# A fused RWKV recurrence and gated MLP on one core: the products of turned k with v cut from 64 to 48 weight columns, the order planned anew, PE gaps filled with longer products of a nearly empty tile, three constants moved to ScalarE

## The chip, the cores and the metric

The kernel runs on one core of a Trainium2 chip. The metric is device time in microseconds, from runs of the whole program. The work is spread over TensorE (PE; its weight loads are listed apart as PEld), VectorE (DVE), ScalarE (ACT), GpSimd (POOL) and the DMA queue of SyncE (SP).

## The reference

```python
def _attn_ref(r, k, v, w, u):
    B, H, S, D = r.shape                      # 4, 8, 768, 48
    state = zeros((B, H, D, D))
    for t in range(S):
        cur = einsum('bhd,bhe->bhde', u[None] * kt, vt)
        y[:, :, t] = einsum('bhd,bhde->bhe', rt, state + cur)
        state = wt[:, :, :, None] * state + einsum('bhd,bhe->bhde', kt, vt)

def _moe_ref(x, w_in, g_ln, w_sg, b_sg, w_out):   # x: (4, 768, 384), the 8 heads side by side
    h = gelu_tanh(x @ w_in)                       # w_in: (384, 1024)
    u, v = h[..., :512], h[..., 512:]
    v_n = (v - mean(v)) / sqrt(var(v) + 1e-6) * g_ln
    v_s = einsum('ts,bsd->btd', w_sg, v_n) + b_sg[None, :, None]   # w_sg: (768, 768)
    return x + (u * v_s) @ w_out                  # w_out: (512, 384)
```

`w_in` and `w_out` come as 64-bit floats and are split on the chip into two 32-bit parts.

## The kernel before

The recurrence is cut into 24 chunks of 128 time steps (4 batches of 6). In a chunk two heads share a tile: a head has 48 channels and takes 64 partitions, so that 16 of each 64 are empty. For each chunk `decays` makes running products of the decays with two scans on DVE (lines 456 and 461), `decays` and `decayed_k` multiply r and k by them (463 and 485, on DVE or POOL), and `turned_k` transposes k on PE (536) and copies it out of PSUM (311, tile `kt`). `own_weights` makes a step's own term (495 and 499 for the first six chunks, 510 to 515 after that) and spreads it over a diagonal into the tile `a` (522 on ACT, 524 on DVE or POOL). `products` makes two things in the PSUM tile `a_ps`: scores of k with r (550) and the turned k with v (553), which is what the chunk adds to the state. `masked` copies the scores into `a` (571, DVE), `state` and `decayed` carry the state on (586, 594, 605), and `outputs` multiplies `a` with v and the state with r (633 and 659), in the PSUM tile `y_ps`. A chunk's products and outputs are 64 by 64 tiles of PE, four side by side; from chunk 6 on the products of the next chunk stand between the two parts of a chunk's outputs.

The MLP follows on each half batch: `v_piece`, `u_piece`, `gate_piece`, `out_piece`, each a run of three products per pair of operands (725, 726, 727), with 128 weight columns and 384 or 512 moving columns.

All instructions are given out by a planner (`Plan`). Each piece of work is a generator that yields `Op`s with a cost per engine and what they wait for. `Plan.run` takes, for each engine, the ops that could start first and among those the one with the lowest rank; ranks are the tables `STEP`, `V`, `U`, `GATE`, `OUT` and `WEIGHT`, and `BIAS` is added to an engine's end when an op may go to several. So the tables fix the order on every engine, and the engine of many element-wise ops. On the chip each engine runs its instructions in this order and waits on semaphores.

Where the planner finds PE idle before 36 us, `keep_warm` puts products there that nobody reads: `ident` by `ident`, 128 columns each, in a PSUM tile that is free (976). At the start POOL makes the constants: `mask`, `diag` (390), `minus` (393) and `same` (394).

Of the kernel before, what the change touches and what calls it, by code (L numbers as in the profile page):

```python
# [38 lines left out]
    -49.59, -15.18, -14.63, -13.68, -11.2, -11.02, 0.94, 1.57, 6.83, 7.5, 7.96, 9.52, 17.35, 17.52, 18.44,  # L39
    20.96, 27.09, 21.08, 30.76, 30.42, 31.57, 41.12, 50.44, 52.07)  # L40
V = (
    -1.34, -0.42, -1.4, -16.57, -17.54, -16.72, -30.2, -1.18, 9.65, 3.42, -39.6, -58.94, -8.2, 47.77, -22.36,
    48.57, 27.83, 112.03, 39.65, 25.41, 38.54, -75.72, 34.43, 84.5)
U = (-10.14, -62.7, 73.58, 25.05, 43.25, -41.51, 3.24, -2.61)
GATE = (-5.38, 7.81, 4.64, 27.34, 89.18, 34.59, 11.76, 26.33)
OUT = (16.92, 42.66, 101.93, 26.86, 133.47, 116.26, 123.25, 158.13)
WEIGHT = {"v": -15.75, "u": -68.31, "sg0": -0.57, "sg1": -9.36, "out": -43.34, "g": 63.42}

HINTED = (mybir.EngineType.PE, mybir.EngineType.DVE, mybir.EngineType.SP)
BIAS = {"DVE": 0.32, "ACT": -0.03, "POOL": 0.34}  # L50
# [4 lines left out]
    (0, 'load_w'): -41.97, (0, 'load_kr'): -41.3, (1, 'load_w'): -38.98, (1, 'load_kr'): -16.05,  # L55
    (0, 'load_v'): -19.51}
# [91 lines left out]
class Plan:  # L148
# [62 lines left out]
    def run(self):  # L211
        while True:
# [13 lines left out]
            for e, c in best.items():  # L226
# [77 lines left out]
def rwkv_gmlp(ctx: ExitStack, tc: tile.TileContext, wpad, kr, vtok, ktok, vt, u, ucol, w_in, g_ln, w_sgT, b_sg, w_out, out):  # L304
# [47 lines left out]
    s_kt = slots("kt", 1, [NP, 128])  # L352
# [25 lines left out]
    nc.vector.memset(D2, 0.0)  # L378
    nc.gpsimd.memset(c.mhalf, -0.5)
# [147 lines left out]
    def turned_k(n):  # L527
# [9 lines left out]
        op = yield Op({"ACT": 0.48, "DVE": 0.58}, take=[s_kt], free=[m_], done=x.e_kt)  # L537
        x.kt, = op.got
        copy(op.e, x.kt.tile[0:m], kt_ps[0:m])

    def products(n, op):
# [9 lines left out]
        for p, c_, j in [(p, c_, j) for p in range(NP) for c_ in range(1 if last else 2) for j in range(2)]:  # L551
            h = 2 * p + j
            nc.tensor.matmul(ps[64 * j:64 * j + 64, c_, NP * T + p * T:NP * T + p * T + D],  # L553
                             kt[64 * c_:64 * c_ + 64, p, 64 * j:64 * j + 64],
# [6 lines left out]
    time = lambda n: {"PE": 0.78 if steps[n][1] == NC - 1 else 1.02}  # L561
# [59 lines left out]
    def outputs(n):  # L621
# [25 lines left out]
        plan.add(rank(n) - 50.0, look(y, e_look, op.seen))  # L647
        if n == N - 1:
# [518 lines left out]
```

## Time and profile before

| | |
|---|---|
| Time, median of 3 runs | 361.45 us (359.83 to 362.5) |
| Profiled execution, its own time | 360.21 us |
| Its span, first to last instruction | 358.5 us |
| PE busy | 346.5 us (97%), 4708 products |
| DVE busy | 274.8 us (77%) |
| ACT busy | 208.6 us (58%) |
| POOL busy | 80.3 us (22%) |
| DMA | 49.81 MB, mean 139 GB/s |

Busy times are those of the profiler; the ends of products are modelled, so the gap from one product's start to the next one's says more than a product's own length. A product of 32-bit floats shows as two records. An engine's idle time is shown with what ended it; "issue" means that the profile shows nothing that the engine waited for.

### The profile page before, as it was taken

The numbers are of one execution on the slowest core, as the hardware profiler recorded it, in microseconds if no ns is written. First come the engines' busy times: TensorE is split into PE (matmuls) and PEld (weight loads), VectorE is DVE, ScalarE is ACT, GpSimd is POOL, SyncE is SP. The second block draws the span as 40 slices with busy tenths as digits, with TensorE's granted clock in tenths as the row PEclk, the third lists the DMA queues.
The fourth block names the chain that finished last, engine by engine and source line by source line (L and its number), as shares of the span: only waits on it lengthen the run. The fifth ranks groups of instructions, "written<-read, shape, count | busy, mean of one in ns | idle before, by whom it ended". The sixth has DMA issues, their size and how long they took to land.

```text
span 358.5 us, 11334 instructions
## 1 busy us (share of the span) xinstructions
PE 346.5 (97%) x4708; PEld 317.4 (89%) x4708; DVE 274.8 (77%) x546; ACT 208.6 (58%) x545; POOL 80.3 (22%) x98
## 2 busy tenths in 40 slices
PE   5899999999999999999999999999999999999995
PEld 5778678898998888989999899998999989999994
DVE  6979998789999999989999877767642527345352
ACT  2868978884456677675644364667562588721010
POOL 7413320123454241443214020105000002000000
PEclk9989999999999999999999999999999999999998
DMA  7867777522466545633563614513224440010101
GB/s 249 307 192 228 233 239 247 163 100 76 115 192 215 186 146 190 205 116 126 157 205 123 199 52 140 160 69 117 102 66 153 133 145 3 0 44 24 44 24 71
DMA packets 23960, 49.81 MB, mean 139 GB/s; under 512 B 3808, under 2 KB 12768, under 8 KB 23904
## 3 DMA queue, kind: packets, MB, share of 16 engines
q1 hardware_dynamic: 23904, 49.04, 42.6%
q8 instruction: 38, 0.62, 0.7%
q14 instruction: 18, 0.15, 0.1%
HBM read 43.12 MB, written 4.72 MB: 133 GB/s over the span
## 4 chain that ended last, share of the span: by engine, by line
PE 69%; DVE 18%; ACT 5%; DMA 4%; issue 2%; SPq 2%; DVEq 0%; ACTq 0%
PE m_ps L725 19%; PE m_ps L727 18%; PE m_ps L726 18%; DVE W L461 3%; PE y_ps L633 3%; PE a_ps L550 3%; PE y_ps L659 2%; DVE W L456 2%; PE a_ps L553 2%; PE m_ps L536 2%; DMA u<-in_w_sgT 2%; SPq L695 2%; DVE a L571 1%; DVE KR L463 1%; DVE m_ps L801 1%
## 5 line engine op out<-in xcount | busy, mean ns | idle before, releaser
L725 PE MATMUL m_ps<-wsgh,vn 128*128 128x384 f32 x192 | 65.6, 341 | 0.0
L727 PE MATMUL m_ps<-wsgh,vn 128*128 128x384 f32 x192 | 64.7, 337 | 0.1
L726 PE MATMUL m_ps<-wsgl,vn 128*128 128x384 f32 x192 | 64.6, 336 | 0.0
L805 ACT CAST g<-m_ps 128x384 fp32r<-128x384 f32 x32 | 15.3, 478 | 41.7 <-DVE m_ps L803 41.7
L756 POOL TENSOR_TENSOR st<-st,mhalf 128x1 f32<-128x1 f32 x24 | 16.5, 687 | 100.0 <-DVE st L754 97.8
L801 DVE SCALAR_TENSOR_TENSOR m_ps<-m_ps,g_ln,b_bc 128x384 f32<-128x384 f32 x32 | 19.6, 620 | 22.5 <-PE m_ps L727 22.5
L725 PEld LDWEIGHTS m_ps<-wsgh,vn 128*128 128x128 f32 x192 | 36.1, 188 | 0.8
L727 PEld LDWEIGHTS m_ps<-wsgh,vn 128*128 128x128 f32 x192 | 36.1, 188 | 0.5 <-DVE vn L767 0.5
L726 PEld LDWEIGHTS m_ps<-wsgl,vn 128*128 128x128 f32 x192 | 36.1, 188 | 0.3
L725 PE MATMUL m_ps<-xT,winh 128*128 128x384 f32 x96 | 33.4, 348 | 0.7 <-ACT u L781 0.7
L725 PE MATMUL m_ps<-g,wouth 128*128 128x384 f32 x96 | 33.1, 345 | 0.0
L472 ACT ACTIVATE junk<-W 128x1032 bf16<-128x1032 f32 x24 | 25.6, 1065 | 12.9 <-DVE W L461 11.4
L726 PE MATMUL m_ps<-xT,winh 128*128 128x384 f32 x96 | 32.3, 337 | 0.0
L727 PE MATMUL m_ps<-xT,winl 128*128 128x384 f32 x96 | 32.3, 337 | 0.0
L726 PE MATMUL m_ps<-g,wouth 128*128 128x384 f32 x96 | 32.2, 336 | 0.0
L727 PE MATMUL m_ps<-g,woutl 128*128 128x384 f32 x96 | 32.2, 336 | 0.0
L456 DVE TENSOR_TENSOR_SCAN W<-W,D 128x516 f32<-128x516 f32 x24 | 29.7, 1236 | 1.7 <-DMA W<-in_wpad 1.7
L461 DVE TENSOR_TENSOR_SCAN W<-W,D 128x516 f32<-128x516 f32 x24 | 30.2, 1259 | 0.2
L725 PE MATMUL m_ps<-winh,xT 128*128 128x512 f32 x72 | 29.9, 415 | 0.0
L727 PE MATMUL m_ps<-winh,xT 128*128 128x512 f32 x72 | 28.5, 396 | 0.0
L726 PE MATMUL m_ps<-winl,xT 128*128 128x512 f32 x72 | 28.4, 395 | 0.0
L485 POOL TENSOR_TENSOR KR<-KR,W 128x512 f32<-128x512 f32 x11 | 17.1, 1557 | 36.6 <-DVE W L456 15.4
(148 smaller groups left out, 826.3 us busy)
## 6 DMA issues: line engine op xcount, KB each, us to landing
KR<-in_kr SPq DMA_DIRECT2D x24, 512.0 KB, 4.3
RK<-in_ktok SPq DMA_DIRECT2D x18, 384.0 KB, 3.5
W<-in_wpad SPq DMA_DIRECT2D x24, 258.5 KB, 3.0
vtok<-in_vtok SPq DMA_DIRECT2D x24, 192.0 KB, 4.4
out<-o SPq DMA_DIRECT2D x21, 192.0 KB, 1.9
vn<-in_w_in SPq DMA_DIRECT2D x6, 512.0 KB, 6.2
KR<-in_w_in SPq DMA_DIRECT2D x6, 512.0 KB, 4.0
u<-in_w_sgT SPq DMA_DIRECT2D x12, 192.0 KB, 4.0
```

What stands on the lines that cost most here:

```text
L456: nc.vector.tensor_tensor_scan(Suf[:, WL - 1:0:-1], W[:, WL - 1:0:-1], D1[:, WL - 1:0:-1], 0.0, ALU.mult, ALU.add)
L461: nc.vector.tensor_tensor_scan(W[:, 0:WL - 1], W[:, 0:WL - 1], D2[:, 0:WL - 1], 0.0, ALU.mult, ALU.add)
L472: nc.scalar.activation(junk.bitcast(BF16).rearrange("p (a x) -> p a x", a=2), both, AF.Square, accum_out=chk[:, n:n + 1])
L485: engine[op.e].tensor_tensor(cols(x.KR[:, 0]), cols(x.KR[:, 0]), blocks(x.Suf, 2), ALU.mult)
L550: nc.tensor.matmul(ps[64 * c_:64 * c_ + 64, j, p * T:(p + 1) * T], k_, r_, start=True, stop=True)
L633: nc.tensor.matmul(place(j, q, r, c_), x.V[64 * c_:64 * c_ + 64, h * D:h * D + 64], x.a.tile[64 * c_:64 * c_ + 64, j, p], start=(start and ...
L725: nc.tensor.matmul(ps, lh, rh, start=(i == 0), stop=False)
L726: nc.tensor.matmul(ps, lh, rl, start=False, stop=False)
L727: nc.tensor.matmul(ps, ll, rh, start=False, stop=(i == n - 1))
L756: nc.gpsimd.tensor_tensor(rstd, var, c.mhalf, ALU.pow)
L801: nc.vector.scalar_tensor_tensor(ps, ps, c.g[:, d:d + 1], c.b_bc[:, ts], ALU.mult, ALU.add)
L805: nc.scalar.copy(gh, ps)
```

## The change

- `products`: the turned k is copied without its empty channels. The tile `kt` holds 2 x 48 columns instead of 128 for each pair of heads, and the product with v has 48 weight columns instead of 64 and writes 48 partitions instead of 64. The rest of that part of `a_ps` is set to zero once, by a memset on DVE at the start.
- The planner's costs follow (0.72 and 0.9 instead of 0.78 and 1.02 for `products`, less for the copy).
- All rank tables are new, and finer: `EARLY` gives each kind of step of chunks 0 to 5 a rank of its own, `TILE` each weight tile. `BIAS` is new, so ops change engines.
- `keep_warm` fills a gap to its end with products of `D1` by `D1` of up to 512 columns in place of `ident` by `ident`. `D1` is zero but for a one in each 129th column. The filling may start at 1.8 us in the plan, not 2.8.
- `diag`, `minus` and `same` are made by ACT in place of POOL.
- The hint for the branch is recorded ahead of the plan; it stands at the same place in the program.

```diff
 STEP = (
-    -49.59, -15.18, -14.63, -13.68, -11.2, -11.02, 0.94, 1.57, 6.83, 7.5, 7.96, 9.52, 17.35, 17.52, 18.44,
...
+    23.46, 56.5, 108.27, 180.81, 64.71, 30.21, 81.2, 85.98, 86.12, 90.4, 103.26, 105.97, 107.42, 110.55, 126.6,
...
+EARLY = {
+    (0, 'decays'): -71.86, (0, 'range_check'): 4.01, (0, 'decayed_k'): -14.94, (0, 'turned_k'): -19.63,
...
+TILE = {
...
-BIAS = {"DVE": 0.32, "ACT": -0.03, "POOL": 0.34}
+BIAS = {"DVE": 0.09, "ACT": -0.33, "POOL": 0.04}
...
-    s_kt = slots("kt", 1, [NP, 128])
+    s_kt = slots("kt", 1, [NP, 2, D])
...
+    nc.vector.memset(m_a.free[0][1][:, :, NP * T:], 0.0)
...
-        nc.gpsimd.tensor_copy(diag[half], ident[half, half])
+        nc.scalar.copy(diag[half], ident[half, half])
...
-    nc.gpsimd.tensor_scalar(minus, ident, -1.0, None, ALU.mult)
-    nc.gpsimd.tensor_copy(same, ident)
+    nc.scalar.activation(minus, ident, AF.Copy, scale=-1.0)
+    nc.scalar.copy(same, ident)
...
-        copy(op.e, x.kt.tile[0:m], kt_ps[0:m])
+        used = kt_ps.rearrange("t p (j d) -> t p j d", d=64)[0:m, :, :, 0:D]
+        copy(op.e, x.kt.tile[0:m], used)
...
-            nc.tensor.matmul(ps[64 * j:64 * j + 64, c_, NP * T + p * T:NP * T + p * T + D],
-                             kt[64 * c_:64 * c_ + 64, p, 64 * j:64 * j + 64],
+            nc.tensor.matmul(ps[64 * j:64 * j + D, c_, NP * T + p * T:NP * T + p * T + D],
+                             kt[64 * c_:64 * c_ + 64, p, j],
                              x.V[64 * c_:64 * c_ + 64, h * D:(h + 1) * D], start=True, stop=True)
...
-    rank = lambda n: STEP[n]
+    rank = lambda n, kind=None: EARLY.get((n, kind), STEP[n])
...
     def keep_warm(t0, t1):
 
-        t0 = max(t0, 2.8)
-        n = int((t1 - t0 - 0.1) / (0.45 if t0 < 5.0 else 0.23))
+        t0 = max(t0, 1.8)
+        per_col = 0.0034 if t0 < 5.0 else 0.0017
         ready = [x for x in m_m.free if x[0] <= t0]
-        if ready and n > 0:
+        while ready and t1 - t0 > 0.12:
             _, m = min(ready, key=lambda x: x[0])
-            for _ in range(n):
-                nc.tensor.matmul(m[:, 0:128], ident, ident, start=True, stop=True)
+            n = min(FF, int((t1 - t0) / per_col) // 32 * 32)
+            nc.tensor.matmul(m[:, 0:n], D1[:, 0:128], D1[:, 0:n], start=True, stop=True)
+            t0 += n * per_col
```

What the new tables do to the order shows at two places. The first is PE between the products of chunk 0 and the first weight tile; `KR_0_82` is chunk 0's k and r, `KR_0_83` chunk 1's, and the rows on `ident` or `D` alone are filling. Before:

```order
L553 MATMUL a_ps_0_127<-vtok_0_85,kt_0_101 64x48 x16
L976 MATMUL m_ps_0_130<-ident 128x128 x4
L633 MATMUL y_ps_0_128<-a_0_98,vtok_0_85 64x64 x8
L536 MATMUL m_ps_0_130<-ident,KR_0_83 128x128 x4
L659 MATMUL y_ps_0_128<-KR_0_82,S_0_105 64x64 x8
L633 MATMUL y_ps_0_128<-a_0_98,vtok_0_85 64x64 x8
L976 MATMUL m_ps_0_131<-ident 128x128 x2
L550 MATMUL a_ps_0_127<-KR_0_83 64x64 x16
L553 MATMUL a_ps_0_127<-vtok_0_86,kt_0_101 64x48 x16
L860 MATMUL m_ps_0_131<-vn_176,ident 128x512
```

The same place on PE now (lines are those of the changed kernel: 582 was 553, 564 was 536, 662 was 633, 579 was 550, 686 was 659, 887 was 860):

```order
L582 MATMUL a_ps_0_127<-vtok_0_85,kt_0_101 48x48 x16
L1002 MATMUL m_ps_0_130<-D_133 128x416
L564 MATMUL m_ps_0_130<-ident,KR_0_83 128x128 x4
L1002 MATMUL m_ps_0_131<-D_133 128x128
L662 MATMUL y_ps_0_128<-a_0_98,vtok_0_85 64x64 x8
L1002 MATMUL m_ps_0_131<-D_133 128x352
L579 MATMUL a_ps_0_127<-KR_0_83 64x64 x16
L582 MATMUL a_ps_0_127<-vtok_0_87,kt_0_101 48x48 x16
L686 MATMUL y_ps_0_128<-KR_0_82,S_0_105 64x64 x8
L662 MATMUL y_ps_0_128<-a_0_98,vtok_0_85 64x64 x8
L1002 MATMUL m_ps_0_131<-D_133 128x384
L887 MATMUL m_ps_0_131<-vn_180,ident 128x512
```

The turning of chunk 1's k and its products now stand ahead of the outputs they stood behind, with more filling between them. The second place is ACT at the same time. Before:

```order
L472 ACTIVATE junk,chk<-W_0_81 128x1032
L311 COPY S_0_105<-a_ps_0_127 128x4x48
L522 ACTIVATE a_0_99<-diag,own_0_91 128x64 x8
L873 CAST winh<-vn_176 128x512
L311 COPY kt_0_101<-m_ps_0_130 128x512
L311 COPY x_0_109<-y_ps_0_128 128x4x128
```

On ACT now (500 was 472, 338 was 311, 634 was 605, 900 was 873, 550 was 522):

```order
L500 ACTIVATE junk,chk<-W_0_81 128x1032
L338 COPY S_0_105<-a_ps_0_127 128x4x48
L338 COPY kt_0_101<-m_ps_0_130 128x384
L634 ACTIVATE S_0_106<-S_0_102,pc_0_94 128x48 x4
L900 CAST winh<-vn_180 128x512
L550 ACTIVATE a_0_99<-diag,own_0_91 128x64 x8
L900 CAST winh<-vn_183 128x512
L338 COPY x_0_109<-y_ps_0_128 128x4x128
```

The copy of chunk 1's turned k has moved ahead of the eight instructions that make its tile `a`.

More of the change, by code (lines that the diff above doesn't have):

```diff
@@ L44 @@
[L44 to L47, printed above, removed]
+    67.13, 59.66, 27.15, 12.56, 18.74, 68.11, 49.03, 38.82, 121.77, 117.09, 50.7, 66.01, 15.93, 137.12, 90.6,
+    35.17, 103.09, 228.31, 182.38, 68.39, 102.46, -37.63, 91.99, 158.21)
+U = (-5.09, -3.83, 197.07, 70.35, 177.67, -109.12, 27.69, 139.75)
@@ L49 @@
+TILE = {
+    "v0": -5.56, "v1": 3.45, "v2": -4.5, "u0": -105.52, "u1": -118.61, "u2": -187.21, "out0": -111.96,
+    "out1": -18.05, "out2": -12.32, "out3": -108.57}
 HINTED = (mybir.EngineType.PE, mybir.EngineType.DVE, mybir.EngineType.SP)
-BIAS = {"DVE": 0.32, "ACT": -0.03, "POOL": 0.34}
+BIAS = {"DVE": 0.09, "ACT": -0.33, "POOL": 0.04}
 JOINED = 6
@@ L54 @@
 FIRST_LOADS = {
-    (0, 'load_w'): -41.97, (0, 'load_kr'): -41.3, (1, 'load_w'): -38.98, (1, 'load_kr'): -16.05,
-    (0, 'load_v'): -19.51}
+    (0, 'load_w'): -191.66, (0, 'load_kr'): -100.08, (1, 'load_w'): -47.22, (1, 'load_kr'): -14.06,
+    (0, 'load_v'): -99.06}
 COLD = 6.0
@@ L225, in run @@
             pick = None
-            for e, c in best.items():
+            for e, c in sorted(best.items()):
                 t0 = min(x[0] for x in c)
@@ L536, in turned_k @@
             nc.tensor.transpose(kt_ps[0:m, p], x.KR[:, 0, p * C:p * C + m], ident)
-        op = yield Op({"ACT": 0.48, "DVE": 0.58}, take=[s_kt], free=[m_], done=x.e_kt)
+        op = yield Op({"ACT": 0.4, "DVE": 0.45}, take=[s_kt], free=[m_], done=x.e_kt)
         x.kt, = op.got
-        copy(op.e, x.kt.tile[0:m], kt_ps[0:m])
+        used = kt_ps.rearrange("t p (j d) -> t p j d", d=64)[0:m, :, :, 0:D]
+        copy(op.e, x.kt.tile[0:m], used)
     def products(n, op):
@@ L560, in rwkv_gmlp @@
     ready = lambda n: [ch[n].e_k, ch[n].e_r, ch[n].e_V, ch[n].e_kt]
-    time = lambda n: {"PE": 0.78 if steps[n][1] == NC - 1 else 1.02}
+    time = lambda n: {"PE": 0.72 if steps[n][1] == NC - 1 else 0.9}
     def first_products(n):
@@ L646, in outputs @@
         e_look = Event()
-        plan.add(rank(n) - 50.0, look(y, e_look, op.seen))
-        if n == N - 1:
-            tc.mark_branch_hint_location("all_right", engines=HINTED)
+        plan.add(rank(n, "outputs") - 50.0, look(y, e_look, op.seen))
         if joined and with_it:
@@ L917, in rwkv_gmlp @@
             weights.append(w)
-            r = WEIGHT[key] + 0.1 * k
+            r = TILE[key + str(k)]
             plan.add(r, f64_weight(*w[1:], e_win[n0][k], r, [s_vn, s_vn], [] if n0 else [ch[0].e_r],
@@ L923, in rwkv_gmlp @@
         weights.append(w)
-        r = WEIGHT["out"] + 0.1 * d
+        r = TILE[f"out{d}"]
         plan.add(r, f64_weight(*w[1:], e_wout[d], r, [s_g, s_g], [ch[5].e_k],
@@ L944, in rwkv_gmlp @@
                 continue
-            plan.add(FIRST_LOADS.get((n, f.__name__), r), f(n))
+            plan.add(FIRST_LOADS.get((n, f.__name__), rank(n, f.__name__)), f(n))
         for f in (decays, range_check, chunk_pc, decayed_k, turned_k, own_weights, first_products, masked, state, decayed,
@@ L949, in rwkv_gmlp @@
                 continue
-            plan.add(r, f(n))
+            plan.add(rank(n, f.__name__), f(n))
     for b in range(B):
@@ L955, in rwkv_gmlp @@
                 for g in range(3):
-                    plan.add(rank(h_.n + g), move(h_, g, g + 1))
+                    plan.add(rank(h_.n + g, "move"), move(h_, g, g + 1))
             else:
-                plan.add(rank(h_.n + 2), move(h_, 0, 3))
+                plan.add(rank(h_.n + 2, "move"), move(h_, 0, 3))
             for g in range(3):
-                plan.add(rank(h_.n + g), split_x(h_, g))
+                plan.add(rank(h_.n + g, "split_x"), split_x(h_, g))
                 plan.add(V[h_.n + g], v_piece(b, 3 * i + g))
@@ L968, in keep_warm @@
     def keep_warm(t0, t1):
-        t0 = max(t0, 2.8)
-        n = int((t1 - t0 - 0.1) / (0.45 if t0 < 5.0 else 0.23))
+        t0 = max(t0, 1.8)
+        per_col = 0.0034 if t0 < 5.0 else 0.0017
         ready = [x for x in m_m.free if x[0] <= t0]
-        if ready and n > 0:
+        while ready and t1 - t0 > 0.12:
             _, m = min(ready, key=lambda x: x[0])
-            for _ in range(n):
-                nc.tensor.matmul(m[:, 0:128], ident, ident, start=True, stop=True)
+            n = min(FF, int((t1 - t0) / per_col) // 32 * 32)
+            nc.tensor.matmul(m[:, 0:n], D1[:, 0:128], D1[:, 0:n], start=True, stop=True)
+            t0 += n * per_col
     plan.keep_warm = keep_warm
+    tc.mark_branch_hint_location("all_right", engines=HINTED)
     with tc.manual_schedule():
```

29 lines of the change are left out of this document (25 added, 4 removed).

## Prediction, made before the changed kernel was run

> **What bounds the kernel now.** I read the page's head first, then the busy time by stretch, the waits, and the start in order of time.
>
> ```profile
> span 358.5 us, 11334 instructions
> PE 346.5 (97%) x4708; PEld 317.4 (89%) x4708; DVE 274.8 (77%) x546; ACT 208.6 (58%) x545; POOL 80.3 (22%) x98
> PEclk9989999999999999999999999999999999999998
> ```
>
> PE is busy nearly throughout. The stretches (length, then busy time with instructions of PE, PEld, DVE, ACT and POOL, the granted clock, DMA) tell where it is not:
>
> ```profile
> 10.00:20.00 10.00, 8.24 (x236) 7.28 (x235) 9.62 (x16) 8.24 (x28) 3.60 (x2) 0.91 0.80 291
> 20.00:30.00 10.00, 10.00 (x142) 7.17 (x138) 8.10 (x14) 7.21 (x24) 1.48 (x1) 0.92 0.61 196
> 40.00:50.00 10.00, 9.52 (x253) 6.97 (x245) 9.24 (x17) 8.10 (x26) 2.10 (x3) 1.00 0.77 236
> 60.00:80.00 20.00, 19.34 (x101) 17.67 (x100) 16.64 (x42) 18.25 (x43) 3.60 (x4) 1.00 0.41 131
> 80.00:100.00 20.00, 19.81 (x273) 18.43 (x272) 19.98 (x38) 9.22 (x24) 8.15 (x7) 1.00 0.33 103
> 100.00:120.00 20.00, 19.18 (x460) 17.91 (x458) 19.93 (x33) 11.84 (x34) 9.69 (x8) 1.00 0.61 193
> 120.00:140.00 20.00, 19.77 (x327) 17.39 (x320) 20.00 (x43) 14.81 (x38) 6.72 (x7) 1.00 0.47 150
> 160.00:180.00 20.00, 20.00 (x338) 19.57 (x327) 19.41 (x39) 11.85 (x30) 5.23 (x6) 1.00 0.48 146
> ```
>
> From 40 to 140 us PE is idle for 0.48 + 0.66 + 0.19 + 0.82 + 0.23 = 2.38 us in all. From 80 to 140 us DVE is never free (19.98, 19.93 and 20.00 of 20), so the two engines are level there: less work on PE alone gains little before 140 us and all of itself behind it. What is left to win by order lies ahead of 40 us. Here is the start on PE, in order of time (start, length):
>
> ```profile
> 8.26 0.64 PE L499 MATMUL m_ps<-u_col,RK 64*64 64x1 f32 x32 [1.01 <-DMA u_col<-in_ucol]
> ...
> 15.67 0.46 PE L659 MATMUL y_ps<-KR,S 64*64 64x64 f32 x16 [0.45 <-DVE look L311]
> ...
> 17.34 0.34 PE L633 MATMUL y_ps<-a,vtok 64*64 64x64 f32 x8 [1.09 <-issue]
> ...
> 18.26 1.13 PE L550 MATMUL a_ps<-KR 64*64 64x64 f32 x32
> ...
> 22.05 0.39 PE L862 MATMUL m_ps<-winl,same 128*128 128x512 f32 x1
> ...
> 25.69 1.02 PE L860 MATMUL m_ps<-vn,ident 128*128 128x512 f32 x2
> ...
> 26.79 0.39 PE L862 MATMUL m_ps<-winl,same 128*128 128x512 f32 x1
> ...
> 29.17 1.50 PE L976 MATMUL m_ps<-ident 128*128 128x128 f32 x12
> 30.60 0.69 PE L550 MATMUL a_ps<-KR 64*64 64x64 f32 x32
> ...
> 31.57 0.61 PE L499 MATMUL m_ps<-u_col,RK 64*64 64x1 f32 x32
> 32.10 0.49 PE L976 MATMUL m_ps<-ident 128*128 128x128 f32 x2
> ```
>
> The first real product starts at 8.26 us, the last filling stands at 32.10 us. Two things are lost between. PE waits 0.45 + 1.09 us near 16 us, the second time for nothing that the profile names. And the clock falls: what stands between 18.26 and 22.05 us (a chunk's products and two thirds of a weight tile, 3.79 us) took 31.57 - 30.60 = 0.97 and 26.79 - 25.69 = 1.10 us elsewhere, so 1.72 us more.
>
> **The change, part by part.** The sum is made against the profiled execution's own 360.21 us (span 358.5 and 1.71 around it).
>
> *Fewer weight columns.* These rows are from the chain of waits in order of time (start, length, what) and from the groups by line:
>
> ```profile
> 31.75 0.44 PE m_ps L499 x31
> ...
> 174.63 0.45 PE a_ps L553 x32
> ```
>
> ```profile
> L726 PEld LDWEIGHTS m_ps<-wsgl,vn 128*128 128x128 f32 x192 | 36.1, 188 | 0.3
> L553 PEld LDWEIGHTS a_ps<-vtok,kt 64*64 64x64 f32 x704 | 13.9, 139 | 0.2 <-ACT kt L311 0.2
> ```
>
> A chunk's 32 products with v take 0.45 us. The moving side is 48 columns before and after; what shrinks is the weights, from 64 columns to 48. Line 499 has 64 weight columns and a single moving one, and its 31 take 0.44 us: the moving side doesn't set the time. A load of 128 columns takes 188 ns, of 64 columns 139 ns, so 49 ns for 64 columns, 0.77 ns each. Four tiles run side by side, so 32 loads are 8 in a row: 8 x 64 x 0.77 = 0.39 of the 0.45 us. With 48 columns 8 x 16 x 0.77 = 0.098 us goes from each full chunk, half of it from the 4 last chunks of a batch, which have only half of these products: 22 x 0.098 = 2.2 us. Ends: 0 (the time is a floor per instruction) and 2.2. I take 2.2, since the lengths of the loads go by columns.
>
> *Changes between tilings.* In the order of PE, runs of 64 by 64 products change with full ones 76 times before and 72 times now. A change there and back costs:
>
> ```profile
> 173.44 0.34 PE L727 MATMUL m_ps<-xT,winl 128*128 128x384 f32 x1
> 173.71 0.46 PE L633 MATMUL y_ps<-a,vtok 64*64 64x64 f32 x16
> ...
> 175.73 0.45 PE L725 MATMUL m_ps<-xT,winh 128*128 128x384 f32 x1
> 176.01 0.34 PE L726 MATMUL m_ps<-xT,winh 128*128 128x384 f32 x1
> ```
>
> In the rows of the end below, products of 384 columns start 0.17 us apart. Here it is 0.27 going in and 0.28 coming back, so 0.2 us for both; two fewer make 0.4 us. All else on PE is the same products in the same number.
>
> *The start.* Filling behind the first real product is 26 products of 128 columns before; the six from 29.17 to 30.60 us take 0.238 us each, so 6.2 us. Now it is 5408 columns in 11 places. A 512-column product of this kind takes 0.86 us (first row below), 1.68 ns a column, so 9.1 us. The old filling and the waits of 0.45 and 1.09 us make 7.7 us together; the new filling claims that room and 1.4 us more. I cost this at nothing, on the ground that filling ahead of a product that waits for DVE or ACT is free; the ends are -2.8 us (the wait of 1.09 and the slow clock's 1.72 both go) and +4.6 us (worked out in the last rival). The copy of chunk 1's turned k moves ahead of the making of `a` on ACT, so chunk 1's products come sooner, but DVE masks them only after its work on the weight tiles, whose order is nearly the same as before.
>
> ```profile
> 25.85 0.86 PE m_ps L860 x2
> ```
>
> The added memset and ScalarE's constants lie in these idle stretches:
>
> ```profile
> 1.07 0.49 DVE L376 MEMSET D<- 128x517 f32 x1 [1.07 <-PEq L1154]
> ...
> 3.80 1.47 DVE L456 TENSOR_TENSOR_SCAN W<-W,D 128x516 f32<-128x516 f32 x1 [1.68 <-DMA W<-in_wpad]
> 6.84 1.06 ACT L472 ACTIVATE junk<-W 128x1032 bf16<-128x1032 f32 x1 [4.75 <-DVE W L461]
> ```
>
> About 0.5 us (517 columns took 0.49) goes into the 1.68 us in which DVE waits for the first decays; without that cover it would delay all by 0.5. Four small ACT instructions go into 4.75 us of waiting. Both cost nothing. The turned k's copy has a quarter fewer elements; ACT isn't what ends last behind 80 us (9.22 of 20 busy), so nothing again.
>
> *Ops on other engines.* Counting the order, DVE gets 7 more of the products of k and r with the decays (40 for 33) and makes 4 fewer of the tiles `a` (8 for 12):
>
> ```profile
> L463 DVE TENSOR_TENSOR KR<-KR,W 128x512 f32<-128x512 f32 x20 | 14.2, 712 | 0.0
> L485 DVE TENSOR_TENSOR KR<-KR,W 128x512 f32<-128x512 f32 x13 | 8.8, 679 | 0.0
> L524 DVE TENSOR_TENSOR a<-own,diag 128x512 f32<-128x512 f32 x12 | 8.2, 680 | 0.0
> ```
>
> 7 x 0.70 - 4 x 0.68 = 2.2 us more on DVE; the other moves add and take about as much. It counts only where DVE is full, which by the stretches above is from 10 to 20 and from 80 to 140 us, 70 of the first 180 us: 2.2 x 70 / 180 = 0.9 us. Ends 0 and 2.2.
>
> *The rest of the order* is new everywhere. It acts on the 2.38 us of PE's waits from 40 to 140 us. Ends: all of it gone, -2.4, or twice as much, +2.4. I take -0.5, close to no change, since with DVE level with PE a wait that goes there mostly comes back at the next step.
>
> Sum: -2.2 - 0.4 + 0 + 0.9 - 0.5 = -2.2, so 358.0 for a profiled execution like this one. The three runs (359.83, 361.45, 362.5) and it have a mean of 361.0, 0.8 above it, and I forecast a median of 358.8 us, 0.7% under 361.45. (1%, 3.6 us, is about what a measurement of this kernel can tell from no change: 357.8 and 365.1.)
>
> **The rivals.**
>
> *The start gains as well.* If the filling and the earlier products close the wait near 16 us, the clock doesn't fall, and 1.09 + 1.72 = 2.8 us go besides: 358.8 - 2.8 = 356.0. For it: DVE itself waits on PE there, as the row below has it, so PE's delay reaches DVE. Against it: nothing shows what the 1.09 us were, so nothing shows that they go.
>
> ```profile
> DVE x L311 <- PE y_ps L633: 1.8, 1, 1.8
> ```
>
> The trace has 9% of one stretch of 10 us missing from the clock and 8% of the next; at half speed that is 1.8 + 1.6 = 3.4 us. The Trainium skill ("TensorE: Matmul & The Clock Gate", Part 1: The HAM clock gate) says that a monitor watches PE in free-running windows of 3413 ns and halves its clock after an idle one; by that rule, and the 3.4 us agree, this rival's 1.72 us go when no window is left mostly idle.
>
> *The loads save nothing.* If 0.45 us is a floor for 32 pairs of load and product, 2.2 us stay: 361.0. For it: 0.44 and 0.45 us are nearly one number, for 1 and 48 moving columns. Against it: the lengths of 139 and 188 ns. The Trainium skill ("TensorEngine Tiling (Array Packing)", Performance Considerations, Instruction Overhead) gives each product an overhead of some 60 cycles, so that one column costs as much as 60; by it the sum would be this rival's. No run so far has 48 weight columns.
>
> *The filling delays the work.* Filling stands in PE's order ahead of real products and can't be passed. If chunk 1 to 4's operands come when they came before, 9.1 - 6.2 = 2.9 us more filling push the products back; and if the wait of 1.09 us falls between the moved products, a second stretch at half clock costs another 1.72. 358.8 + 4.6 = 363.4, slower than before. It decides where a filling ends later than what the product behind it waits for. For it: the new filling is 1.4 us longer than all the room seen. Against it: the planner's cost, 1.7 ns a column, is what the trace shows.
>
> **How the numbers follow.** Forecast 0.50, the start gains 0.22, the loads save nothing 0.13, the filling delays 0.15. The forecast alone spans about 356.8 to 360.6 (0 to 2.2 on DVE, and an order better or worse by 1). The range runs from 355.0, a little beyond the start's gain, to 362.8, just short of the filling's price: it leaves out about 0.18. Faster by over 1% is the start's gain (0.21 of it) and the low fifth of the forecast and a little more (0.19): 0.40. Slower by over 1% is the worst of the filling with a worse order: 0.10. Within 1%: 0.50.
>
> **What would show it.** The 32 products with v should take about 0.35 us from the first's start to the next row's (right), or 0.45 (the loads save nothing). The clock in the stretches from 10 to 30 us should stay below 1.00 (forecast) or reach it (the start gains). Fillings followed at once by products that had long been released would show the last rival. DVE should stay at 19 or more of 20 from 80 to 140 us. The end must be the same: its last products of 384 columns come 0.17 us apart, as here:
>
> ```profile
> 353.62 0.33 PE L726 MATMUL m_ps<-g,wouth 128*128 128x384 f32 x1
> 353.79 0.33 PE L727 MATMUL m_ps<-g,woutl 128*128 128x384 f32 x1
> ```
>
> Waits on PE of over 3 us anywhere behind 40 us would make the prediction wrong.

## The result, and the profile after

The changed kernel takes 365.26 us (median of 6 runs, 363.8 to 368.09) against 360.64 us of the kernel before in the same runs: the ratio is 1.0148, with a 95% interval of 1.0109 to 1.0188. The profiled execution took 365.04 us, 1.7 us of it outside the span. The forecast was 358.8 us, so the change made the kernel slower where a small gain or nothing had been expected. Medians here hold every run; ratios and their intervals leave out the single executions that were over 1.5% slower than the fastest of the same kernel.

The page of the changed kernel: span, busy times, the granted clock over 40 slices of the span, the queue that carries instructions (packets, MB, share), and the shares of the chain that ended last.

```profile
span 363.3 us, 11275 instructions
PE 347.4 (96%) x4674; PEld 312.3 (86%) x4674; DVE 273.9 (75%) x549; ACT 211.4 (58%) x564; POOL 79.0 (22%) x92
PEclk9999998999999999999999999999999999999998
q8 instruction: 38, 0.62, 0.7%
PE 94%; DVE 2%; issue 2%; POOL 0%; ACT 0%; DVEq 0%
```

TensorE's busy time is nearly what it was (347.4 against 346.5 us). DVE works as long as before, and the chain is TensorE's own to 94%. So the loss isn't an engine that has become the bound. The stretches (length, busy time with instructions of PE, PEld, DVE, ACT, POOL, granted clock, DMA share, GB/s) show where it lies:

```profile
10.00:20.00 10.00, 9.59 (x234) 6.70 (x233) 8.26 (x16) 8.23 (x29) 3.12 (x2) 1.00 0.63 233
20.00:30.00 10.00, 10.00 (x140) 6.24 (x142) 9.66 (x18) 8.18 (x27) 1.48 (x1) 1.00 0.74 253
40.00:50.00 10.00, 8.57 (x245) 6.38 (x244) 9.88 (x19) 8.91 (x28) 2.14 (x4) 1.00 0.79 236
50.00:60.00 10.00, 7.68 (x151) 5.94 (x150) 5.60 (x13) 4.89 (x13) 3.73 (x4) 0.98 0.65 220
60.00:80.00 20.00, 20.00 (x141) 18.18 (x140) 16.36 (x41) 14.98 (x35) 1.84 (x2) 0.93 0.46 154
80.00:100.00 20.00, 19.45 (x171) 18.61 (x170) 19.54 (x41) 10.38 (x26) 6.36 (x6) 1.00 0.17 51
120.00:140.00 20.00, 19.90 (x428) 17.45 (x431) 19.74 (x39) 16.33 (x49) 4.82 (x6) 1.00 0.58 185
200.00:220.00 20.00, 18.09 (x422) 16.54 (x421) 17.65 (x30) 11.53 (x38) 2.68 (x4) 1.00 0.70 227
```

The start has what the kernel before lacked: a full clock from 10 to 30 us (0.91 and 0.92 before). But TensorE is idle for 1.43 us from 40 to 50, 2.32 us from 50 to 60 and 1.91 us from 200 to 220 us, where it lost 0.48 us, nothing and nothing before, and the clock now falls behind the second of these. The waits by engine, line and releaser (us in total, times, longest) name no one:

```profile
PE a_ps L582 <- issue: 2.6, 2, 2.1
PE m_ps L754 <- issue: 1.9, 1, 1.9
PE m_ps L527 <- issue: 1.4, 1, 1.4
PE y_ps L662 <- issue: 0.2, 1, 0.2
```

"Issue" is a wait for nothing that the profile shows: 6.1 us, where the kernel before had one such wait of 1.09 us. In order of time (start, length, what, wait ahead of it and its releaser):

```profile
47.36 0.59 PE L527 MATMUL m_ps<-u_col,RK 64*64 64x1 f32 x31
49.38 0.16 PE L527 MATMUL m_ps<-u_col,RK 64*64 64x1 f32 x1 [1.43 <-issue]
...
55.03 0.52 PE L582 MATMUL a_ps<-vtok,kt 64*48 64x48 f32 x14
57.69 0.24 PE L582 MATMUL a_ps<-vtok,kt 64*48 64x48 f32 x2 [2.15 <-issue]
...
214.87 0.34 PE L753 MATMUL m_ps<-wsgl,vn 128*128 128x384 f32 x1
217.12 0.34 PE L754 MATMUL m_ps<-wsgh,vn 128*128 128x384 f32 x1 [1.92 <-issue]
```

Each wait cuts through a row of like products on the same operands: 31 of 32 had run, 14 of 16, two of the three passes of one accumulation. Nobody can have been waited for there. What lies at these places is a border of the instruction stream itself. The 38 packets of the instruction queue hold 0.62 MB, 16 KB each, and 4674 products with as many loads are 9348 instructions of about 66 bytes (0.62 MB / 9348), so a packet holds some 250 instructions, or 125 products with their loads. Number TensorE's products in order as the trace counts them, from 0, filling included (an f32 product counts twice); the expectations call these numbers records. The wait of both kernels near 17 us falls at product 220, and the three large new ones at 854, 981 and 3399: the last two steps are 127 and 19 times 127.3. Semaphore waits and a few other instructions stand in the same stream. With them counted in, as the trace holds them, the five issue waits of the changed kernel (its 0.2 us at L662 is one) stand multiples of 256 instructions apart, to within one (449, 1728, 1984, 3521 and 6848). So do 45 of the 46 issue waits of all 16 traces; the one that doesn't is 0.48 us at 9.76 us in the run with 32-column filling. These borders are called crossings below; product 220 is the first at which TensorE waits, and 35 of them follow in each kernel. The fetch for a crossing can be seen, too. In the bulk of 49.9 to 55.2 us the DMA view of the changed kernel has no instruction packet; in the 0.2 us from 55.2 to 55.4 us, when TensorE runs dry, it has one:

```profile
q1 hardware_dynamic: 41, 0.07, 90.5%
q8 instruction: 1, 0.02, 28.6%
```

TensorE goes on 2.4 us after that packet starts (55.29 to 57.69). The other fetches start at 47.07 and 214.44 us and TensorE resumes at 49.38 and 217.12, so 2.3 to 2.7 us each (2.2 to 3.0 in all runs). Each crossing is followed by one packet, which brings the code behind the next: the packet of 47.07 us belongs to the crossing of 46.01 us, and TensorE waits for it at the crossing of 49.38 us.

Between the two profiled executions the span grew by 4.8 us. The first real product starts 0.36 us later (8.62 for 8.26). From the start of the last product, the one of the closing count, to the end of the span it is 1.83 us more (356.98 to 363.26, against 354.05 to 358.50). What lies between grew by 2.57 us: +5.0 of issue waits, -2.1 of other waits (2.9 before, 0.8 now, behind the first product), -2.1 of weight loads (an estimate, from the check of that term below), +3.3 of filling (from each filling's start to the next product's start: 7.0 and 10.3 us), and the half clock about even (10 x 0.09 + 10 x 0.08 = 1.7 us lost before, 10 x 0.02 + 20 x 0.07 = 1.6 now). These make 4.0; the rest, -1.4, I don't divide.

The theory that I tested first: TensorE waits where its stream crosses into 16 KB that were fetched too late, and the change has moved the crossings to bad places by having 34 products fewer in its filling (4674 for 4708). The rivals: the waits belong to the new order; the filling stands on the path; the narrower loads lost something.

### The profile page after: what moved, and what is told of

It reads as the page before. It is cut to its first block, busy times and chain, and to the rows that moved or that the text cites. A ratio compares the mean times of both kernels' runs of the same rounds, so it can differ in the third digit from the quotient of the medians.

```text
span 363.3 us, 11275 instructions
## 1 busy us (share of the span) xinstructions
PE 347.4 (96%) x4674; PEld 312.3 (86%) x4674; DVE 273.9 (75%) x549; ACT 211.4 (58%) x564; POOL 79.0 (22%) x92
## 4 chain that ended last, share of the span: by engine, by line
PE 94%; DVE 2%; issue 2%; POOL 0%; ACT 0%; DVEq 0%
PE m_ps L752 24%; PE m_ps L754 23%; PE m_ps L753 23%; PE m_ps L1002 5%; PE y_ps L662 4%; PE a_ps L579 3%; PE m_ps L564 3%; PE y_ps L686 3%; PE a_ps L582 2%; PE m_ps L887 2%; PE m_ps L527 1%; DVE m_ps L828 0%; PE m_ps L889 0%; PE m_ps L888 0%; PE m_ps L741 0%
## 5 line engine op out<-in xcount | busy, mean ns | idle before, releaser
L754 PE MATMUL m_ps<-wsgh,vn 128*128 128x384 f32 x192 | 64.6, 336 | 1.9 <-issue 1.9
L783 POOL TENSOR_TENSOR st<-st,mhalf 128x1 f32<-128x1 f32 x24 | 22.1, 922 | 122.0 <-DVE st L781 113.5
L754 PEld LDWEIGHTS m_ps<-wsgh,vn 128*128 128x128 f32 x192 | 36.1, 188 | 0.0
L484 DVE TENSOR_TENSOR_SCAN W<-W,D 128x516 f32<-128x516 f32 x24 | 32.5, 1354 | 1.1 <-DMA W<-in_wpad 1.1
L754 PE MATMUL m_ps<-xT,winl 128*128 128x384 f32 x96 | 32.5, 339 | 0.0
L754 PE MATMUL m_ps<-g,woutl 128*128 128x384 f32 x96 | 32.2, 336 | 0.0
L489 DVE TENSOR_TENSOR_SCAN W<-W,D 128x516 f32<-128x516 f32 x24 | 30.0, 1251 | 0.1
L754 PE MATMUL m_ps<-winh,xT 128*128 128x512 f32 x72 | 28.5, 396 | 0.0
L834 DVE TENSOR_TENSOR g<-m_ps,g 128x384 fp32r<-128x384 f32 x32 | 17.4, 548 | 7.0 <-ACT g L832 6.7
```

The lines of the kernel that those rows point to most:

```text
L484: nc.vector.tensor_tensor_scan(Suf[:, WL - 1:0:-1], W[:, WL - 1:0:-1], D1[:, WL - 1:0:-1], 0.0, ALU.mult, ALU.add)
L489: nc.vector.tensor_tensor_scan(W[:, 0:WL - 1], W[:, 0:WL - 1], D2[:, 0:WL - 1], 0.0, ALU.mult, ALU.add)
L754: nc.tensor.matmul(ps, ll, rh, start=False, stop=(i == n - 1))
L783: nc.gpsimd.tensor_tensor(rstd, var, c.mhalf, ALU.pow)
L834: nc.vector.tensor_tensor(g.tile[:, 1], ps, gh.bitcast(F32), ALU.subtract)
```

## Experiments

Ratios are to the kernel before, run on the same chip in turn.

**Moving the crossings.** The first filling, which ends at about 8.6 us in the changed kernel, is given out in more and smaller products. What follows is untouched.

```
-  # 3 products of 512 columns, 1 of 192
+  for _ in range(47):                     # shift40: 22
+      nc.tensor.matmul(m[0:32, 0:16], D1[:, 0:32], D1[:, 0:16], start=True, stop=True)
+  for _ in range(1):                      # shift40: 2
+      nc.tensor.matmul(m, D1[:, 0:128], D1[:, 0:FF], start=True, stop=True)
```

> The changed kernel, but the zeros' products that fill TensorE before the first real work are given out as 47 tiny products (32 by 16) and one of 512 columns, so that 88 more product records stand ahead of the rest of TensorE's program and nothing behind them is altered. Theory A (the stalls without a cause at 47.8, 55.3 and 214.9 us lie where TensorE's instruction stream crosses into its next 16 KB, and the fetch of that piece comes late): the crossings lie 88 products earlier in the work, at the changed kernel's times of about 46.6, 53.6 and 212.8 or 225.5 us instead of 49.4, 57.7 and 217.1; the stalls leave the products at which they stand now (the attention products behind records 856, 983 and 3399), and appear, if anywhere, ahead of products 88 records earlier; time 358 to 365 us, around 361. Rival B (the stalls belong to those products themselves, a wait that the records don't show): they stay at the same products, and the time stays at 365 us within 1.

> The changed kernel, but the filling before the first real work is given out as 22 tiny products (32 by 16) and two of 512 columns: 40 more product records stand ahead of the rest. Theory A (late fetches of the instruction stream): the crossings lie 40 products earlier, at the changed kernel's 47.3, 54.7, 213.4 us; the stall of 2.15 us at 55.3 us stands then ahead of a product 40 records earlier, the one at 214.9 us has gone from its place, a stall at 16.9 us has moved or gone; time 360 to 365 us. Rival B (the products' own waits): the same stalls at the same products, 365 us within 1.

With 88 more: 362.85 us, ratio 1.0076 (1.0046 to 1.0105). The waits have no issue row any more, and the view's granted clock is 1.00 in every stretch up to 300 us (the last section says why that isn't so at the start). It is that fast although the real work starts later: the tiny products didn't bring the clock up, the filling behind the first real product ran at half its speed, and the first products with v began at 17.69 us instead of 13.02. With 40 more: 361.49 us, 1.0023 (0.9997 to 1.0049), and what is left of the issue waits:

```profile
PE a_ps L582 <- issue: 1.5, 2, 1.1
PE m_ps L754 <- issue: 0.2, 1, 0.2
```

The products that waited in the changed kernel no longer do; those that wait now stand at crossings. The rival that the waits belong to the order is out: order and operands are the same here.

The end also moved back: from the start of the last product to the end of the span it is 4.4 us in both (355.58 to 360.0, 356.97 to 361.4), 6.3 in the changed kernel. The trace shows where: TensorE's branch behind the closing count lasts 3.89 us in the changed kernel (358.33 to 362.22), with a packet of code that starts at 359.86 us, and 0.39 us in the kernel before, 0.40 with 40 more.

**Sixty more, with the clock up.** To the edit with 40 more, 10 tiny products are added in the second filling, in place of half of its first product.

> The changed kernel with 60 more product records ahead of the work: the first filling as 22 tiny products and two of 512 columns (so that the clock rises as it did in the run with 40 more), and 10 tiny products in the second filling in place of half of its first product. Counting pieces of 16 KB of TensorE's instructions, at 1.0 us from a crossing to the next fetch and 2.6 us for the fetch, the changed kernel as it is has 5.8 us of stalls by its own times, the one with 40 more about 1.5 to 3, the one with 60 more 0.3, and the kernel before none behind its first. Theory A: 359 to 361 us, TensorE's waits on nothing that the profile shows under 1 us in all, and the end after the last product back at 4.2 us (6.1 in the changed kernel). Rival B (the 40 more were luck of another kind): 361.5 to 365 us.

361.14 us, ratio 1.0013 (0.9976 to 1.0049); issue waits 1.2 us in all, 0.2 over what was expected:

```profile
PE y_ps L662 <- issue: 0.9, 1, 0.9
PE y_ps L686 <- issue: 0.3, 1, 0.3
```

Against 1.0148 this is 1.35% or 4.9 us, and the two intervals lie apart, though order and operands are the changed kernel's. So the place of the crossings explains the loss, and with them out of the way the change as a whole is worth nothing that can be measured. The forecast of 0.7% less lies outside this interval: the gain doesn't appear either.

**The end alone.** 30 products more stand ahead of the last 36 of the last stage.

```
+  if d == 0 and b == B - 1 and half == 1 and i == 0:
+      for _ in range(15):
+          nc.tensor.matmul(ps[0:32, 0:16], D1[:, 0:32], D1[:, 0:16], start=True, stop=True)
   mm3_part(ps, ((c.wout_h[:, d, ms], c.wout_l[:, d, ms]), (g.tile[:, 0], g.tile[:, 1])), d, FT)
```

> The changed kernel with 30 more product records (15 tiny products, about 0.5 us) ahead of the last 36 products of its last stage and nothing else altered. In the changed kernel a crossing of 16 KB of TensorE's instructions falls on record 4671 of 4674, and the time from the last product to the end is 6.1 us against 4.2 before. Theory A (the code of the end waits for a fetch that this crossing starts too late): the crossing lies 30 records, about 5 us, ahead of the end, and the end after the last product comes back to 4.2 us: 363.5 to 364.5 us, with the stalls at 47.8, 55.3 and 214.9 us as they were. Rival G (the longer end has another cause: the order, the last output's transfer): 6.1 us there and 365.5 to 366 us.

The end is back, as theory A had it:

```profile
span 363.8 us, 11334 instructions
...
359.41 0.19 PE L1024 MATMUL m_ps<-junk,ones 128*1 128x1 f32 x2
```

363.8 - 359.41 = 4.4 us, and the branch lasts 0.48 us. The three large waits stayed (0.9, 2.3 and 1.2 us at L527, L582 and L754), a new one of 0.9 us stands at L662. The time, 365.2 us and 1.0124 (1.0064 to 1.0183), can't be told from the changed kernel's: the gain at the end is there in the trace and not in the time. Waits for other engines and loads are 2.2 us behind the first product, 0.8 in the changed kernel, and issue waits 5.3 for 6.1; what took up the rest isn't divided.

**A bad place for the kernel before.** Its first filling becomes 11 tiny products and 8 of 128 columns, 18 more.

> The kernel before, with nothing altered but the filling ahead of the first real product: 11 tiny products and 8 of 128 columns for 10 of 128, 18 product records more in about the same time. Theory A (the place of the crossings alone costs microseconds): counted as above, the kernel before has no stall behind its first 20 us as it stands, and 3.4 us of them with 18 more records, 1.6 of it at about 138 us and 1.2 at about 232 us: 362.5 to 364.5 us. Rival B (the stalls belong to the changed order): 360.6 us within 1.

360.21 us, ratio 0.9997 (0.9969 to 1.0026): the size was wrong. Waits do appear at the two crossings named, near 138 and 230 us, but they are a fifth of the forecast:

```profile
PE y_ps L633 <- issue: 0.6, 2, 0.3
```

And the wait of 1.09 us at 17 us went away as the crossing moved. (Its start differs in one more way: products ran at half speed up to about 12.4 us.) So a rule of "1.0 us to the fetch and 2.6 us for it" counts too much; a dense piece alone costs some 0.3 us here. In the changed kernel the wait of 1.43 us has a piece used up in 1.9 us (46.01 to 47.95), its fetch starting 1.05 us behind the crossing. The two longer waits, of 2.15 and 1.92 us, have fetches that start 5.9 and 3.7 us behind theirs (49.38 to 55.29, 210.72 to 214.44): something makes these start late.

**What delays a fetch.** In the ten traces so far, the time from a crossing to the start of its fetch was 0.3 us in the median where fewer than 4 DMA packets were in flight at the crossing (147 crossings), and 1.2 us in the median and up to 6.3 us where 12 or more were (173). To see whether the loads do it, zeros are written to parts of the output that later get their real values; TensorE's program is that of the changed kernel.

```
   nc.sync.dma_start(raw, src)                       # a load of output weights
+  if rank == TILE["out3"]:
+      for b in range(2):
+          nc.sync.dma_start(out[b, 0:256, 0:HALF].rearrange("(m p) t -> p m t", p=128),
+                            D1[:, 0:HALF].unsqueeze(1).broadcast_to([128, 2, HALF]))
```

> The changed kernel with its TensorE program untouched, and 768 KB more of transfers behind the second load of the output weights, issued at about 50.8 us: two writes of zeros into parts of the output that are written again later. Theory A2 (the fetch of TensorE's next 16 KB waits in the DMA engines behind the loads queued there, which in the changed kernel keep all 16 busy from 46 to 55.5 us): the loads drain 3 to 4 us later, the fetch that starts at 55.3 us starts at about 59, and the stall of 2.15 us ahead of record 983 becomes 5 to 6 us; the time 367 to 369 us. Rival F (the fetch starts late for a reason of its own, or the stall is no fetch): the stall stays at 2.1 us within 0.4, and what is added is at most some waits for x's moves.

> The changed kernel with its TensorE program untouched, and 768 KB of zeros written into parts of the output that are written again later, issued at about 47.6 us, so ahead of the crossing at 49.5 us. If a fetch queues in the DMA engines behind what was issued before its request: the fetch that starts at 47.1 or the one at 55.3 us starts 1.5 to 3 us later, and the waits of TensorE at 47.8 and 55.3 us, 3.6 us together, become 5 to 7 us. If what was issued before does not matter: 3.6 us within 0.7.

> The changed kernel with its TensorE program untouched, and 2.3 MB of zeros written into parts of the output that are written again later, issued from about 243.4 us, where the DMA engines are idle. The next crossing is at 246.1 us, the fetch starts at 247.2 us, and the crossing at 249.6 us (record 3780) finds it just landed: no wait now. If a fetch queues behind transfers issued before it: the transfers last to about 249.5 us, the fetch starts 2 to 3 us later and TensorE waits 2 to 3 us for nothing that the profile shows ahead of record 3780. If not: the fetch starts at 247.2 us within 0.7 and there is no such wait; then only waits for the loads of k and r, which come later too.

The first one issued its transfers from 52.75 us on, behind the crossing at 49.10 us: the fetch still started at 55.47 us, the wait was 2.5 us, and the time 367.59 us (2 runs, 1.0213, interval 1.0132 to 1.0294). That is the time which theory A2 named, without its wait of 5 to 6 us. The bulk did last to 60 us, so a fetch doesn't wait until everything has drained. The second was to add them at 47.6 us, but SyncE was held up ahead of them and issued them at 49.2 us only, with the next loads behind. The crossing came at 50.11 us, its fetch at 57.01 us, the waits at the two places were 1.3 and 2.0 us (365.48 us, one run). The fetch is 6.9 us behind its crossing, within the spread of the runs that add nothing ahead of it, so this decides nothing.

The third is clearer, though it is one run. The writes went out from 245.47 us in a quiet stretch. The crossing comes at 247.83 us, and its fetch starts only at 251.21 us, 3.4 us later (0.7 to 1.3 us in the changed kernel and the five other runs with this placing). TensorE stands still at the products at which it had not waited before, and then runs at half speed for some 3 us:

```profile
251.08 0.54 PE L686 MATMUL y_ps<-KR,S 64*64 64x64 f32 x24
253.49 0.29 PE L686 MATMUL y_ps<-KR,S 64*64 64x64 f32 x5 [1.86 <-issue]
...
255.77 0.52 PE L753 MATMUL m_ps<-wsgl,vn 128*128 128x384 f32 x1
256.09 0.52 PE L754 MATMUL m_ps<-wsgh,vn 128*128 128x384 f32 x1
```

Products of 384 columns start 0.32 us apart there, 0.17 elsewhere. Three of the four writes were issued by then, at 245.47, 245.95 and 246.52 us; their 3 x 0.58 MB, at the 0.36 MB/us at which the DMA engines moved data there from 245.8 us on, last to about 250.6 us. So a fetch that queues behind what was issued before it, and not behind what comes later, fits this run and the first. What this does not explain is why the fetch at 55 us starts 5.8 to 7.9 us after its crossing in all runs with this placing of the crossings, whatever is loaded ahead: that stays open. The run took 369.94 us, 4.5 more than the 365.48 of the run beside it with the other writes, but not all of that is due to these writes: at 247 us this run was already 0.9 us behind the other, with a wait of 3.7 us for code at 59.38 us, long before them.

**The filling.** Each product of it from 7 us on has 32 columns instead of up to 512, in the same places; then half the columns, with the crossings 60 products earlier.

```
-  nc.tensor.matmul(m[:, 0:n], D1[:, 0:128], D1[:, 0:n], start=True, stop=True)
+  w = n if t0 < 7.0 else 32               # shift60_half: w = max(32, n // 64 * 32)
+  nc.tensor.matmul(m[:, 0:w], D1[:, 0:128], D1[:, 0:w], start=True, stop=True)
```

> The changed kernel, but every zeros' product of the filling behind the first real work has 32 columns instead of 512, the same number of instructions in the same places. Theory C (the filling stands on the path: 10.5 us of it against 7.0 before, and TensorE is never waiting for anyone else): up to 9 us less filling; part of it comes back as waits for the engines that feed TensorE, and part as a lower clock in 10 to 30 us; 356 to 362 us, and idle time of TensorE appears between 8 and 36 us. Rival D (the filling lies in time in which TensorE would wait anyway): 364 to 368 us, the filling's time turned into waits. The stalls at crossings of the instruction stream stay at the same records by theory A.

> The kernel with 60 more records, but each filling behind the first real product has half its columns, in the same number of instructions. Theory C (filling beyond what keeps the clock up stands on the path): 10.5 us of filling become about 5.5; if the clock stays up, 2 to 4 us less than with whole filling, the rest coming back as waits for the engines that feed TensorE. Rival E (this filling is what holds the clock): half the clock for some microseconds between 10 and 30 us, as with 32 columns, and the time the same or up to 4 us more. Rival D (waits would stand there anyway): the same time within 0.7 us.

With 32 columns it is slower yet, 368.39 us, ratio 1.0249 (1.0211 to 1.0286). Theory C had allowed for a lower clock at the start, but neither theory for one that costs more than the filling saves: the filling is what holds the clock.

```profile
10.00:20.00 10.00, 10.00 (x228) 8.99 (x227) 8.57 (x16) 7.54 (x26) 3.50 (x2) 0.53 0.64 222
```

Granted clock 0.53 from 10 to 20 us, 0.92 from 50 to 60 and 0.96 from 60 to 80 us. The crossings being the same, the waits stand at the same products (1.1, 2.2 and 1.2 us). With half the columns: 360.49 us, ratio 1.0001 (0.9965 to 1.0038), against 1.0013 with whole filling, which can't be told apart. Filling fell by 4 us (10.6 to 6.6 by the starts) and the profiled span by 0.9. Part of what was saved went into the clock, as rival E had it, only later than it said:

```profile
30.00:40.00 10.00, 9.27 (x118) 5.75 (x117) 9.97 (x19) 8.38 (x26) 4.80 (x2) 0.83 0.75 234
```

That stretch has 1.00 with whole filling; 0.17 of 10 us is 1.7 us. So 4 us less filling are worth about a microsecond as things stand, taken back by the clock and by waits; how much by each, these runs don't tell.

The run with 88 more and half the filling puts both together:

> The changed kernel with 88 more product records as in the run with 88, but 40 of them ahead of the work with two products of 512 columns behind them (so that the clock is up at the first real product, 4.7 us earlier than in that run) and 48 in the second filling, and with half the columns in each later filling. By theory A the crossings lie where the run with 88 more had no wait without a cause: no such wait over 0.5 us, and by the stages of that run and of the one with half the filling 359 to 361 us, against 361.1 and 360.5 of the two with 60 more. If the place of the crossings decides little beside the feeding of TensorE: 360.5 us within 0.7, with new waits.

361.91 us, ratio 1.003 (0.9991 to 1.0069). No issue wait, as expected, but the clock was not up at the first real product: the 32 products with v took 0.80 us at 17.50 us, and the trace's clock records begin at 20.71 us only. And there is a new wait for a transfer at about 30 us, with half the clock behind it for 3.4 us:

```profile
PE m_ps L741 <- DMA x<-x: 2.9, 1, 2.9
```

**The narrower weights.** The changed kernel with k's copy and the products with v as before (64 weight columns), and the kernel before with the narrow ones alone.

```
-  nc.tensor.matmul(ps[64 * j:64 * j + D, c_, ...], kt[64 * c_:64 * c_ + 64, p, j], ...)
+  nc.tensor.matmul(ps[64 * j:64 * j + 64, c_, ...], kt[64 * c_:64 * c_ + 64, p, 64 * j:64 * j + 64], ...)
```

> The changed kernel with its order, its filling and its zeroing, but k's turned copy keeps its empty channels and the products with v load 64 columns of weights as before. If the narrower load is worth what the prediction reckoned (22 times 0.098 us) and is not given back by the late fetches: 2.1 us more than the changed kernel, 367 to 368 us. If the denser stream of instructions is what makes the fetches late (one part of theory A: a piece of 128 product pairs is used up in about 2 us where products are small): the stalls are smaller, and the time is 364 to 366 us. If the loads are worth nothing: 365 us within 0.7.

> The kernel before with its own order, and of the change only k's copy without the empty channels, the products with v 48 by 48, and the one zeroing that they need; the number of TensorE's instructions is the same. By the prediction's first term: 22 times 0.098 us less, 358.0 to 359.0 us. If loads of fewer columns save nothing, or the time is made up by waits or late fetches: 360.6 us within 0.7.

With 64 columns again the changed kernel takes 367.12 us, ratio 1.0212 (1.0175 to 1.0248) against 1.0148 (the intervals overlap a little): 0.64% or 2.3 us more. The same products take 0.46 us there:

```profile
30.40 0.63 PE L581 MATMUL a_ps<-vtok,kt 64*64 64x48 f32 x32
30.86 0.61 PE L527 MATMUL m_ps<-u_col,RK 64*64 64x1 f32 x32
```

Its issue waits are 3.9 us for 6.1, as the second reading wanted, but its time isn't that reading's. The narrow weights alone, in the kernel before, give 359.54 us, ratio 0.9961 (0.9925 to 0.9997), 1.3 us less in the medians and short of the 358 to 359 expected. In its profiled execution (361.13 us, above the median, with half the clock from 16.1 to 22.9 us) there are more waits for other engines than in the kernel before, this one the longest:

```profile
PE y_ps L661 <- ACT a L523: 1.3, 1, 1.3
```

**Both gains on the old order.** The narrow weights and the 18 products more in the first filling.

> The kernel before in its own order, with the two edits that each ran alone: k's copy without the empty channels with the products with v 48 by 48, and 18 more product records in the first filling (which took away the stall of 1.1 us at 16 us). If the two add up: 1.3 and 0.6 us less than before, 358.5 to 359.2 us, and faster than both kernels. If the shorter products only make the feeding engines late: 360 us within 0.6.

358.54 us (357.56 to 359.63) beside 360.02 of the kernel before: ratio 0.9965 (0.9942 to 0.9989). It has the lowest median of all, faster than both kernels, and keeps of the change only the 48 columns, with their copy and zeroing. By the ratios it can't be told from the narrow weights alone (0.9961), and the 18 products alone gave 0.9997, so the gain that is shown is that of the weights.

## Why the prediction was wrong

*Fewer weight columns*, -2.2 us: right in mechanism. The 32 products take 0.36 us to the next row's start, as the first check wanted:

```profile
30.23 0.54 PE L582 MATMUL a_ps<-vtok,kt 64*48 64x48 f32 x32
30.59 0.61 PE L527 MATMUL m_ps<-u_col,RK 64*64 64x1 f32 x32
```

Taking the edit back cost 2.3 us in the medians, and the edit alone gained 1.3. The rival by which the loads save nothing is out: the time followed the weight columns. The overhead of some 60 cycles for each product, by which one moving column costs as much as 60 (the Trainium skill, "TensorEngine Tiling (Array Packing)", Instruction Overhead), is therefore not what sets the time of these products.

*Changes between tilings*, -0.4 us: no run took it by itself.

*The start*, 0 with ends of -2.8 and +4.6: the term's size held. The clock did what the rival "the start gains as well" asked for (1.00 from 10 to 30 us), and the filling grew by 3.3 us for the 2.9 reckoned. Up to 50 us, the time that TensorE spends on anything but its own products at full pace (filling, waits, half speed) is about 0.8 us more than before, an estimate from the starts of all products, less what like products take where nothing waits. The two nearly cancelled. The half clock of the kernel before, by the clock records, stood from 18.21 to 21.63 us, behind a stretch of equal length with 1.54 us of idle, so that stretch was not "mostly idle" as the rival had it.

*The filling delays the work*, the rival at 363.4 us, came nearest in time, by luck: its mechanism was wrong. Half the filling saved 0.65 us in the medians, within the noise, and 32 columns cost 3.1.

*Other engines' work*, +0.9 us: not seen. DVE stayed at 19.54, 19.68 and 19.74 of 20 from 80 to 140 us, as the check had it, but TensorE lost only 0.82 us there against 1.24 before.

*The rest of the order*, -0.5 with ends of 2.4 either way: TensorE's waits from 40 to 140 us are 4.57 us for 2.38, nearly the end on the bad side, but 3.58 of it are the two large issue waits. No run shows that the order itself is better or worse.

The step that failed is the treatment of the wait of 1.09 us "for nothing that the profile names". The prediction left it as one loss at the start, to go or to stay with the clock. It was one of 36 places at which TensorE can wait for its own code, and the sum had no term for the 35 others. In the changed kernel that term is +5.0 us of issue waits, +1.8 us at the end, and part of the 1.6 us at half clock around 60 us. The last check, that waits of over 3 us behind 40 us would make the prediction wrong, is what happened: 5.7 us of issue waits in all. "The end must be the same" failed too, for the same reason. Whether the order of the kernel before is less prone to these waits isn't known: with its own placing it has 1.1 us of them, with 18 products more 0.6.

The crossings are not the whole of it. With them moved, the change comes to 1.0013 and not to the 0.7% gain of the forecast. 1.2 us of issue waits remain there, and no run divides the rest.

The Trainium skill describes this ("Runtime: NRT & Kernel Launch", Instruction fetch mechanics): each engine's code comes in blocks of 16 KiB or 256 instructions, fetched while the one before runs, and hidden by the pace of issue. The blocks agree with the 256 instructions between the waits here. That the fetch is hidden does not: a piece of small products is used up in as little as 1.9 us (46.01 to 47.95 us), and TensorE goes on 2.2 to 3.0 us after a fetch starts, which itself can come up to 8 us behind its crossing. The same section says that a taken branch whose target is outside the held blocks stalls. The trace agrees as far as it goes: the branch at the end lasts 3.89 us where a crossing falls on the last three products and 0.39 to 0.48 us in the three traces named above where it doesn't.

## What to carry to other kernels

Where a tuned kernel waits in the middle of a row of like products for "issue", count instructions: a few cheap ones added ahead of everything show in one run whether the place of the instruction blocks is the cause, and must be ruled out before an order is judged by its time. A change of order is to be compared over several such placings, since here one order took 361.1 or 365.3 us, by 60 products in its filling. Short weights' loads are priced by their columns, and filling is priced by whether the clock holds without it.

## What was not expected of the hardware

A wait of 2 us of TensorE for its code can cost up to 1.6 us again in clock: behind the wait at 55 us in the changed kernel the granted clock was 0.98 and 0.93, and behind the one made at 251 us products came 0.32 instead of 0.17 us apart for about 3 us. It need not: behind the wait of 1.92 us at 217 us the granted clock stayed at 1.00. 94 products of 32 by 16 in the first 5.2 us, in place of wide ones, did not raise the clock: the 512-column filling at 10.90 us behind them took 4.10 us for 6, 2.15 us in the changed kernel. The view of the granted clock reads 1.00 there, which is a trap: it takes off only what a clock record tells, and in that trace the first record starts at 17.08 us (8.30 in the changed kernel). Lengths of products have to be compared for the time ahead of it. And the fetches of code share the DMA engines with the kernel's own transfers: in one run some 1.7 MB of writes issued just ahead delayed one by about 2.3 us.
